# Transposing x in pairs of chunks: two chunks to a PSUM bank, one copy for both, and a new order of all steps

## The chip, the core and the metric

The kernel runs on one core of one Trainium2 chip. The metric is the device time of one execution in microseconds. Three runs of the kernel before took 796.67, 796.89 and 797.10 us. The profile is of one further execution, which took 797.87 us; between its first and last instruction lie 796.0 us. The granted TensorE clock was 1.000 throughout.

The engines are called as in the profile: PE is TensorE (PEld its loads of weights), ACT is ScalarE, DVE is VectorE, POOL is GpSimd, SP is the engine that issues the DMAs.

## What is computed

```python
B, S, D = 1, 2048, 640
xn = layernorm(x)                               # over the last axis
# A: attention with 32 heads of width 20
qkv = xn @ wqkv                                 # [640, 1920]
scores = einsum("bhqd,bhkd->bhqk", q, k) * 20 ** -0.5
s = (softmax(scores) @ v) @ wo
# B: a mixer with two MLPs
h = gelu(layernorm(xn) @ w1)                    # four column groups, shifted by 1, -1, 2, -2 tokens
x1 = xn + shifted(h) @ w2
b = x1 + gelu(layernorm(x1) @ w3) @ w4          # w3 is [640, 1536]
out = x + s * silu(b)
```

All inputs and the output are bfloat16.

## The kernel before

**Tiles.** The 2048 tokens are 16 tiles of 128 tokens, and four chunks `c` (or groups `g`) of 512. The 640 columns of x are five chunks of 128, `kc` 0 to 4. The heads are handled in eight "quads" of four heads, each with four query chunks `qc`. For one quad and query chunk the scores of a key tile are formed for two heads at a time in two PSUM banks (a "score pair", `sc{quad}_{qc}_{tile}_{0 or 1}`, line 1596 or 1609), ACT takes the exponential of the 128x1024 block (`exp...`, line 1656), and PE multiplies the result with the values (`pv...`, lines 1389 and 1588). For a part of the key tiles DVE computes the exponential instead, in bits: `u...` (line 1680) and the pieces `s...` (line 1576, some on POOL, line 1574). The branch B (`w1`, `w2`, `w3`, `w4`), the projections for the next heads (`s1_`, `s0_`) and the final product with `wo` (`woa`, `wob`) are laid into the attention as further PE work whose results DVE evacuates (line 725 is the helper for all of these products).

**A score pair has two forms.** In its row form it is two matmuls of 32 rows by 128 columns (line 1596), in its column form eight of 128 by 32 (line 1609). `follow` (line 218) chooses for the steps that are marked `flex`: the row form when the PE step before is in row form, or the next one is row or flex.

**The order.** `program` only lists the steps. Which engine runs which step when, and which PSUM bank and which buffer each one gets, stands in the string `TABLE`: two characters name a step, and one more character follows for each bank or buffer that it takes. `follow` reads it, keeps the order of the steps of each engine, and adds waits for the buffers. Durations and latencies in the list of steps (`dlat`, `C_SP` and the like) change nothing in the instructions that are emitted except, at most, which of several implied waits is written down.

**PSUM.** Seven banks are handed out: single ones as "W" (for transposes, projections, `wo`), pairs as "S" (score pairs for ACT), any two as "S2" (for DVE). Bank 7 collects the attention output.

**The start.** x is loaded and normalised (DVE, ACT and POOL share the tiles). PE transposes x on itself: for a group of four tiles and a chunk `kc`, sixteen matmuls of 128x128 (line 1076, steps `tr_x{g}_{kc}_{tile}` of four matmuls each) fill half a PSUM bank with 512 bfloat16 columns, and one copy (line 1085, steps `trev_x{g}_{kc}`) brings them to `xnT`:

```python
for kc in range(0, 0 if g in cfg.TD else cfg.KC, cfg.TP):
    h, wa = self.wtile()
    act = bk in cfg.TRA
    bk += 1
    nk = min(cfg.TP, cfg.KC - kc)
...
    def fe(e, d=d, h=h, nk=nk, act=act):
        p = self.wbank(h, BF16)[:, 0:512 * nk].rearrange("p (k n) -> p k n", k=nk)
        return e.activation(d, p, AF.Copy) if act else e.tensor_copy(d, p)
```

`cfg.TP` is 1, so there are 20 such banks and copies, numbered `bk` 0 to 19; `cfg.TRA` lists the 14 that ACT copies, DVE copies six. The key projection of group c, `KT_c` (five steps of four matmuls), needs the chunks of group c alone. DVE takes its largest absolute value (`mx_c`, line 1177) and ACT brings it to SBUF (`kev_c`, line 1180). Only when all four are there, DVE combines the maxima (`mx_`, `mq_`, lines 1192 and 1194), and PE adds the bound to the queries (`sh_0`, line 1161; `qad_0`, line 1167). Then come the first score pair and the first exponential. Until the first chunks are there, PE runs 41 fillers (`warm`, line 898).

**The end.** The last query chunk of the last quad is done in two halves of 256 queries (`sh0_`, `sh1_` are its score pairs, lines 1467 and 1471; `exph0_`, `exph1_` their exponentials; `uh0_`, `uh1_` DVE's, line 1506). The rows of the output that wait for the last quad alone are `wob8` to `wob15` (line 1827), each filling two banks which DVE empties (line 1834). `keep_busy` (line 1411) lays filler matmuls into PE's queue there, 29 steps; `cfg.FLN` lists their form (0: four matmuls, 1: two in row form) and number.

Of the kernel before, what the change touches and what calls it, by code (L numbers as in the profile page):

```python
# [472 lines left out]
class Cfg:  # L473
# [5 lines left out]
    def __init__(self, S=2048, D=640, H=32, F=1536):  # L479
# [48 lines left out]
        self.OND = 100.0  # L528
        self.TP = 1
# [125 lines left out]
class Gen:  # L655
# [29 lines left out]
    def A(self, name, *key):  # L685
        a = (name,) + key
        self.pl.own(name, a)
        return a
# [1337 lines left out]
    def b_w3(self, c0):  # L2026
# [8 lines left out]
        for ch in (c0, c0 + 1):  # L2035
# [12 lines left out]
            for fc in range(FC):  # L2048
# [3 lines left out]
                  writes=[A("W3s", ws)], is_dma=True, nbytes=KC * 128 * 128 * 2, name=f"ld_w3_{ch}_{fc}", stream=f"w3{ws}")  # L2052
# [16 lines left out]
    def b_w4(self, n0, n1):  # L2069
# [6 lines left out]
        for hh in range(2):  # L2076
            hs = slice(hh * HALF, (hh + 1) * HALF)
            T("sp", C_SP, lambda e, hs=hs: e.dma_start(W4[:, :, :], w4src[:, :, hs]),
              writes=[A("W4")], is_dma=True, nbytes=FC * 128 * D, dlat=800.0, name=f"ld_w4_{n0 // 4}_{hh}", stream="w4")
# [27 lines left out]
    r"#6#9#0#y#:###,#$#-$@$K$V#f#(#)$)#;#<#=#>#%#e$b#&#?#@#A#B#C&c#'#*&d#.#D#E#F$*#G$2#H$+$,#I$-$.#n#}#~$/#J$##K$0#g$3$4%5)#z#{#|#L#M#N#+#O#P#Q#d#R$$#S#s$%%"  # L2107
    r":##r$5#k$c#T$&#p#o#U#t#V$'#W$6#X#q#Y#u#i#Z$M$P$d$1$L#v#w#x$n$$o$p$s%$x(#m%&&%'%($($}'$~$t$u$7$v$8$9$N%#%$$:$O$;%%$Q$q$r$e$g$<$R$?%)$w#h#[$D#]$y#^$z$E$"
    r"{#_%*#`$|#a&b#b&e$%w%%x$f$>$A&l'&m&z&%y%z&{$B$F&n$S$C%{&o%+(&p$=$h$G$i#j$Z&|$X%|&}$H%6%7%8%9%,%;%<%=$W&~%>%-&f%.&g%/%0%&h&i%1$[#l%2$j%3%4$I$k%?)%@%A$]"
    r"%~#$Y%B%C&#$T$l#c$^$J&$&%&&$U%X%$_%Y%N(%O%P%S)%Z%[%]%T%U&q%V$m%D'%E'#&)&&j&*%I$%Q&+(X%F%G%W%J&,%K$`%c%%R%H$a%L&-%^)%_%`%a%h(%d%i%j&'%e%f%k%b#2%r'%s%l%"  # L2110
    r"t%u%m)%n%o%p%M&0$&1&2&3&4%g%v%q&.&7%&8%}&/&9(Y&5&:&6&;'+'&<','-'.'/&O&&>&?&@&('0&F$&D(#8&G&H&E1l&I&J&K*:&*;%&P&Q&=*G(*<)*H#*>*=&R&S*J$*@/&T*B*K$*?(*A%"
    r"&s&&t&u&v&w*L%&X)&Y*E(*M&*C&x&y#/*P+*S*R&Z&[&]'u*F'*T%*N*V('%#'&&^&_*k(''*l&*U**h%*W'(')*i$*D*m(*n)*I'1&'2'*'8#*O%'9*Q%&A&L':';'<*X#5*f('=*g#&U&M)&N+A"
    r"'3*r%*s''4'5*o+%&*z(#7'6'7*j'Y&'Z'[']'^+&)*[&`('$&a*{#'K''L'M*p&*q$*e'N'O*|('?(*}&'@'A'_'>'P*w#+#&'B+$%'C*_&V%*x('D&W'R$'S'T'U'V*~'W+($+)#+C'+F*Y*]+E+"
    r"/#*t+0&+4(+5$+H$'E#+J'F'G*b'H+K+*#++''I*c1m'J&C+'+-$+9(+:)'f#'g'h'i*^+,'j'k+.%'l*u#+S(*Z+V+U'`#'a'b'c+7$'d*v#*y+G#'e+8'+X(+Z'm#+I#+[&B+M$*a'n+1(W+t#+w"
    r"(Z+N(+2(+3%'o'p'q+B$'r's+O(+v+y/+6+{*d+D&+;+R$+W#+P$+Y)*`+T%([+|'t'v#'w'x+<,V+=+k(+i#'y'z+Q+j'+b+l$'|('}'{'~(#($+s#+x&+L+h+z(+u)(%(&%('+m,-4,'&((()(*,"
    r"(#+_,/'X,G#,H&+d(+(,((-+~&,0,2(,#$,)#,5,*'(.(/,4(0.},$&,%%(1(3+}+],c#,D((^((2+e+f(_+`+g,E)+>+^,+(a,d(&r,X&,Z+n(+o#,B#,C',&+c+a,^$,I(,J$,>,6,[+p#,F,a,7"
    r"+q%,L',`,1$(5$(6(7(8,;,K,=(9,3),i#,,$,@,M',8,:,N'(:'Q,?+r,.$,<,]$+?+@,l,O&,k,n1,q,_#,p,A,m',o),P(](`,9,Q(;$-)$,W#,Y$(<,t-*%(=,r(>(?(@,s,e#,R,h',b,w,j&"
    r",f#,u,z(A((B,v--6-9'-0-:$(C(D(E-'#-j-(',},g-$'-/-26(F-4(G(-%)(H(j-1#-3#-5(I)*(J(K-7(-8&-<&-+-=%(k&(l(m(L-B%-E-D,~(-#',{(n(o(p->&,|.7%-G(-I-&-?(.8)-;,y"
    r"-J-,&-M(M-.&-@,x-P-A#-F(-L(d((e-H$(f(c(P-C%(g(h(i-K-W&(b(4-6-Q)+&(N),)--X'-Z%-[#).)/)0-N-l&-n-`(-a&-O-Y-V-o-b#-q$-t-s-R-]((O#-c$-^'(Q-p#-S-d(R-T-|$-~-"
# [115 lines left out]
```

## Time and profile before

| | |
|---|---|
| median of three runs | 796.89 us |
| the profiled execution | 797.87 us, its span 796.0 us |
| PE busy | 776.3 us (98%) |
| ACT busy | 766.7 us (96%), of which line 1656 676.4 us |
| DVE busy | 730.8 us (92%) |
| POOL busy | 354.5 us (45%) |
| copies of the transposed x on ACT (line 1085) | 14, 7.4 us |
| copies of the transposed x on DVE (line 1085) | 6, 2.3 us |

Busy time of PE is modelled from pipelined matmuls, and overlapping ones make it look full; whether PE waits is read from the waits of its weight loads (PEld). A row of the timeline gives start, length, engine, line, operation, tiles and count, then in brackets the idle time before it and what ended that. In the rows of waits the three numbers are the total, the count and the longest wait.

### The profile page before, as it was taken

What the parts mean: (1) busy time and instruction counts of PE and PEld (TensorE: products, weight loads), DVE (VectorE), ACT (ScalarE), POOL (GpSimd) and SP (SyncE); (2) the same over time, 40 slices, a digit from 0 to 9 for tenths busy, and PEclk for the clock granted to TensorE, in tenths of its full rate; (3) what the DMA queues carried; (4) which work ended last, traced back from release to release, by engine and by line L of the source; (5) the groups of instructions that cost most, each with busy time, mean ns of one, the idle gap of its engine ahead of it and who ended that gap; (6) DMA issues with size and microseconds to landing.
All of it is one profiled execution on the core that took longest, in us unless ns stands there. A gap on an engine that the chain in (4) does not pass through costs nothing.

```text
span 796.0 us, 29830 instructions
## 1 busy us (share of the span) xinstructions
PE 776.3 (98%) x13369; PEld 322.5 (41%) x13369; DVE 730.8 (92%) x1206; ACT 766.7 (96%) x802; POOL 354.5 (45%) x208
## 2 busy tenths in 40 slices
PE   9999999999999999999989999999999999999997
PEld 4433333334444333333534444334333343435454
DVE  8889899999999999999998999999988888999967
ACT  7899999999999999999999999999999999999994
POOL 5464234242546737663443442544232443442553
PEclk9999999999999999999999999999999999999999
DMA  5013552444031214335141143314242112133522
GB/s 166 11 24 82 132 121 63 109 111 92 9 68 37 48 40 81 84 75 102 37 101 44 23 104 54 79 43 85 57 97 67 21 43 67 24 91 82 144 90 85
DMA packets 138671, 57.58 MB, mean 72 GB/s; under 512 B 111040, under 2 KB 133744, under 8 KB 138544
## 3 DMA queue, kind: packets, MB, share of 16 engines
q1 hardware_dynamic: 138544, 55.68, 30.2%
q8 instruction: 105, 1.72, 0.9%
q14 instruction: 22, 0.18, 0.1%
HBM read 34.70 MB, written 10.33 MB: 57 GB/s over the span
## 4 chain that ended last, share of the span: by engine, by line
ACT 55%; PE 40%; DVE 3%; issue 1%; DMA 0%; SPq 0%; DVEq 0%
ACT arena L1656 47%; PE psum L725 13%; PE psum L1596 9%; PE psum L1588 6%; PE psum L1389 5%; PE psum L1609 4%; ACT arena L2063 3%; ACT arena L1638 2%; PE psum L898 2%; DVE arena L1680 1%; ACT arena L1971 1%; ACT arena L2091 1%; PE psum L1076 1%; PE psum L1467 1%; ACT L1656 0%
## 5 line engine op out<-in xcount | busy, mean ns | idle before, releaser
L1656 ACT ACTIVATE arena<-psum 128x1024 bf16<-128x1024 f32 x726 | 676.4, 1040 | 13.8 <-PE psum L1596 8.5
L1680 DVE TENSOR_SCALAR arena<-psum 128x512 uint16<-128x512 f32 x536 | 341.6, 682 | 27.9 <-PE psum L1596 24.3
L1574 POOL TENSOR_TENSOR arena<-arena 128x2048 int32<-128x2048 int32 x68 | 244.5, 3599 | 263.8 <-DVE arena L1576 178.7
L725 PE MATMUL psum<-arena 128*32 128x320 bf16 (+1 forms) x5776 | 327.5, 332 | 2.1 <-DVE arena L1576 1.7
L1596 PE MATMUL psum<-arena 32*128 32x512 bf16 x1642 | 197.2, 384 | 7.7 <-ACT arena L1656 4.5
L725 PEld LDWEIGHTS psum<-arena 128*32 128x32 bf16 x5776 | 140.4, 96 | 121.1 <-issue 26.3
L1588 PE MATMUL psum<-arena 128*22 128x512 bf16 x2144 | 183.5, 381 | 1.0 <-DVE arena L1708 0.9
L1576 DVE TENSOR_SCALAR arena<-arena 128x4096 uint16<-128x4096 uint16 (+1 forms) x151 | 161.3, 1090 | 3.7 <-PE psum L1588 2.9
L1389 PE MATMUL psum<-arena 128*22 128x512 bf16 x1448 | 137.8, 381 | 0.3 <-DVE arena L1708 0.2
L1596 PEld LDWEIGHTS psum<-arena 32*128 32x128 bf16 x1642 | 55.0, 91 | 177.8 <-ACT arena L1656 97.5
L1609 PE MATMUL psum<-arena 128*32 128x512 bf16 x1368 | 104.1, 381 | 0.1
L1588 PEld LDWEIGHTS psum<-arena 128*22 128x22 bf16 x2144 | 50.0, 91 | 61.3 <-issue 29.4
L1716 POOL TENSOR_TENSOR arena<-arena 128x512 bf16<-128x512 f32 x30 | 40.9, 1363 | 63.3 <-DVE arena L1576 45.9
L1389 PEld LDWEIGHTS psum<-arena 128*22 128x22 bf16 x1448 | 35.7, 90 | 48.0 <-issue 24.4
L1609 PEld LDWEIGHTS psum<-arena 128*32 128x32 bf16 x1368 | 28.6, 95 | 34.6 <-ACT arena L1656 25.3
L2056 DVE CAST arena<-psum 128x512 bf16<-128x512 f32 x48 | 32.7, 683 | 3.9 <-PE psum L725 3.4
L1265 DVE CAST arena<-psum 128x512 bf16<-128x512 f32 x40 | 26.9, 684 | 1.7 <-PE psum L725 1.2
L1638 ACT ACTIVATE arena<-psum 128x2048 bf16<-128x2048 f32 x13 | 24.5, 1888 | 0.6 <-PE psum L1596 0.6
L937 DVE BATCH_NORM_STATS2 arena<-arena 128x6 f32<-128x320 bf16 x54 | 24.3, 478 | 0.7 <-DMA arena<-in_A_x_dram 0.7
L954 POOL TENSOR_SCALAR arena<-arena 128x640 bf16<-128x640 bf16 x16 | 14.0, 877 | 24.2 <-DVE arena L1576 20.2
L1708 DVE STREAM_TRANSPOSE arena<-psum 128x512 f32<-128x512 f32 x31 | 22.0, 709 | 1.4 <-PE psum L1588 1.4
L2063 ACT ACTIVATE arena<-arena 128x6144 bf16<-128x6144 bf16 x4 | 21.1, 5315 | 0.0
(125 smaller groups left out, 360.4 us busy)
## 6 DMA issues: line engine op xcount, KB each, us to landing
arena<-in_B_w_dram SPq DMA_DIRECT2D x48, 160.0 KB, 2.8
arena<-arena SPq DMA_DIRECT2D x124, 32.0 KB, 1.9
arena<-in_B_w_dram SPq DMA_DIRECT2D x4, 960.0 KB, 6.6
arena<-in_A_x_dram SPq DMA_DIRECT2D x8, 320.0 KB, 5.8
arena<-in_A_x_dram SPq DMA_DIRECT2D x16, 160.0 KB, 2.5
out_dram<-arena SPq DMA_DIRECT2D x16, 160.0 KB, 2.0
heads<-arena SPq DMA_DIRECT2D x120, 20.0 KB, 2.0
arena<-queries SPq DMA_DIRECT2D x28, 80.0 KB
```

The costliest lines, as they stand in the source:

```text
L725: ins = e.matmul(pb[32 * c:32 * c + 32, 0:N], lhsT(k, c), rhs(k, c), start=(k == 0), stop=(stop and k == nk - 1), tile_position=(0, 32 * c))
L1389: ins = e.matmul(pb[32 * i:32 * i + 22, 0:512], VA[:, ql, kts[i // 2], i, :], PT[:, slots[i // 2][0].slot, 512 * (i % 2):512 * (i % 2) + 512],
L1574: return e.tensor_tensor(dst.bitcast(I32), U[:, ub, 0:w].bitcast(I32), bass.AP(c.tensor, c.offset, [list(c.ap[0]), [0, w // 2]]), op=ALU.add)
L1576: fa if onp else lambda e, v=v, dst=dst: e.tensor_scalar(dst, U[:, ub, 0:w], EXP_B[v], None, op0=ALU.add),
L1588: ins = e.matmul(pb[32 * i:32 * i + 22, 0:512], wv, dst[:, at:at + 512].bitcast(BF16), start=first, stop=final, tile_position=(0, 32 * i))
L1596: return e.matmul(out, self.KT[32 * i:32 * i + 32, b, 128 * kt:128 * kt + 128], self.QT[32 * i:32 * i + 32, b, 512 * qc:512 * qc + 512], s ...
L1609: ins = e.matmul(out[32 * c:32 * c + 32, :], self.KT[:, b, 128 * kt + 32 * c:128 * kt + 32 * c + 32], self.QM[:, gb, 2 * a + jj, :], start ...
L1638: lambda e: e.activation(self.PT[:, hp[0].slot:hp[0].slot + 2, :], self.psum[:, 512 * h0.slot:512 * h0.slot + 2048].rearrange("p (a b) -> ...
L1656: lambda e: e.activation(self.PT[:, hp.slot, :], self.psum[:, 512 * hs.slot:512 * hs.slot + 1024], AF.Exp, scale=cfg.scale),
L1680: lambda e, k=k, h=h: e.tensor_scalar(U[:, ub, 1024 * at + 512 * k:1024 * at + 512 * k + 512], self.bank(h.slot)[:, :], a_exp, EXP_BIAS, o ...
L1716: return e.tensor_tensor(OnT.rearrange("p (k d a) -> p a k d", k=4, a=4), Ob[:, :].rearrange("p (a k d) -> p a k d", a=4, k=4), in1, op=AL ...
L2063: T("act", c_act(FC * 512), lambda e, G=G, i=i: e.activation(G[:, i, :, :], G[:, i, :, :], AF.Gelu_apprx_tanh), reads=gta, writes=gta, nam ...
```

## The change

- `TP` becomes 2: in each group the chunks 0 and 1, and 2 and 3, share a bank, and one copy of 128x1024 takes both to SBUF; chunk 4 keeps a bank and a 128x512 copy of its own. 12 copies are left, `bk` 0 to 11. `TRA` gives 1 to 8 of them to ACT (five of 1024 columns, three of 512), so DVE has `trev_x0_0` and the three of group 3 (three of 1024, one of 512).
- `FLN` lists 31 fillers in place of 29, in other forms.
- `TABLE` is another string: every engine's queue is ordered anew, and banks and buffers are handed out anew. Apart from the copies and the fillers, the steps are the same.
- `W3L`, `W4L` and `OND` are latencies that stand in the list of steps; the first two keep their values.

```diff
@@ class Cfg
         self.OND = 100.0
+        self.W3L = 0.0
+        self.W4L = 800.0
         self.TP = 1
...
         self.OQ = 1800.0
+        self.OND = 800.0
         self.WF = True
-        self.FLN = tuple( [(0, 1), (0, 2), (1, 3), (0, 5), (1, 2), (1, 2), (1, 3), (0, 11)])
+        self.TP = 2
+        self.TRA = [1, 2, 3, 4, 5, 6, 7, 8]
+        self.FLN = tuple( [(0, 2), (1, 4), (0, 3), (1, 2), (1, 2), (1, 3), (1, 1), (0, 3), (0, 11)])
...
@@ b_w3, b_w4
-                  ..., is_dma=True, nbytes=KC * 128 * 128 * 2, name=f"ld_w3_{ch}_{fc}", stream=f"w3{ws}")
+                  ..., is_dma=True, nbytes=KC * 128 * 128 * 2, dlat=cfg.W3L, name=f"ld_w3_{ch}_{fc}", stream=f"w3{ws}")
...
-              ..., is_dma=True, nbytes=FC * 128 * D, dlat=800.0, name=f"ld_w4_{n0 // 4}_{hh}", stream="w4")
+              ..., is_dma=True, nbytes=FC * 128 * D, dlat=cfg.W4L, name=f"ld_w4_{n0 // 4}_{hh}", stream="w4")
...
@@ TABLE: every line of the string but the first few characters differs
```

The queues of the start, read from the two strings (banks are not shown, and stretches that don't matter here are left out; `x0_4` and the like after the first of a run are `trev_x0_4` and so on):

```
ACT before  trev_x0_1 x0_4 x0_2 | sxx15 norm6 norm5 qev_0 | trev_x1_2 x1_3 x1_0 x1_1 x1_4 | norm14 | trev_x2_4 x2_3 x2_2 x2_0 x2_1 | trev_x3_3 | kev_1 kev_2 kev_0 kev_3 | exp...
ACT after   trev_x0_4 x0_2 | sxx15 norm6 norm5 qev_0 | trev_x1_4 | norm14 | trev_x1_0 x1_2 | trev_x2_4 x2_0 x2_2 | kev_0 kev_1 kev_2 kev_3 | exp...
DVE before  ... norm12 norm13 mx_0 | trev_x3_0 qbias x3_2 x3_1 x3_4 | mx_1 aq_0 ve2 mx_2 mx_3 mx_ mq_ vev0_5 qad_0 ...
DVE after   ... mx_0 norm12 norm13 vev0_3 | trev_x3_2 x3_4 x3_0 | aq_0 mx_1 mx_2 mx_3 mx_ mq_ qbias vev0_5 qad_0 ...
PE before   ... KT_1 and the transposes of groups 2 and 3, mixed; KT_2 KT_3 | v0_5 | QT_2_0 QT_1_0 | sh_0 ...
PE after    ... transposes of group 2 | KT_1_0 to KT_1_3 | transposes of group 3 | KT_1_4 KT_2 KT_3 | QT_1_0 QT_1_1 v0_5 QT_1_2 | sh_0 ...
```

In the middle, all queues keep their broad course (the same exponentials, the Gelu and the output steps come after the same number of exponentials to within a few) and differ in the fine order nearly everywhere.

The queue of PE at the end, from the score pairs of the last half on, with the pair of banks each takes:

```
before   sh1_14a1:[3,4] sh1_14a0:[0,1] wob8:[3,4] sh1_12a0:[0,1] sh1_1d1:[3,4] wob9:[0,1] sh1_12a1:[3,4] sh1_10a0:[0,1] wob10:[3,4] wob11:[0,1] sh0_8a0:[3,4] sh1_1d0:[0,1] sh0_8a1:[3,4] sh1_10a1:[0,1] ...
after    sh1_14a0:[5,6] sh1_14a1:[0,1] wob8:[5,6] sh1_12a0:[0,1] sh1_1d1:[5,6] sh1_12a1:[0,1] wob9:[5,6] wob10:[0,1] sh1_10a0:[5,6] wob11:[0,1] sh0_8a0:[5,6] sh1_1d0:[0,1] sh0_8a1:[5,6] sh1_8a1:[0,1] ...
```

More of the change, by code (lines that the diff above doesn't have):

```diff
@@ L2111 @@
[L2111 to L2114, printed above, removed]
@@ L2199 @@
[L2199 to L2200 removed]
+    r"$)#9#,$@#y#6$K&Z#%##&[#&#f$2$1$b$3#(#)#-#.#$#e$*#'#:#;$+$,$-#<#=#>#*#?#@#z#A#B#C#g#D$.#}$4#E#F$/#G#+#H#d#{#I#n#J#K$0#L%)##~#|#k$##M#N$$#s#O#P$%#p#Q$&$"
+    r"(#r#i#R#S$5$6$c$'#o$7#T$d#t#q#l#U#/$P#V#W#X#u#v#Y$M$L#Z#[#]#^#_$8#`$9#w%$$#x$w%$:$n&$N$;%%$o$O$p#h$e$x$E%&%'$q$r$s$t$y$z${%($|$Q$g$u$R$}$<$S$~$v%#$B#m"
@@ new lines @@
+    r"R)dx)bSa.a'd1#d)e1d2#d7'd3%bL$bTd8$bUbMbNbVbWbObPbQd5#d6&dyc~d-&cJd.'a(`tc}cNa5bZa6cKeP#eQ)d+d*d9d&d'eA&d#eR(eS$d(d4bb&eB&bcb['bdbee+bfbgeC(bXbjb]b^b_"
+    r"eD#b`e9&bYe:%d%bad/eEeJ#eL(d$eK#eM&bq#brbsbh^*e.btbubz)b{bve7#b|b}bye8(d:bib~c#eN#e<(e='edbk)d;ble(d<e>#bmbnbobpey(e?)ez$e,d>d?e{#eOc$)e*d=d^(c%c&c'c("
+    r"e|#e;bwd_c)et#eV(eWeu(c*d@dAdBdCev#e/ew&db(e@e0e'e}df#dceo(ep)d`c+e)ddexdedgdhdDdEdFdj#dkdle-dibxdme2(e3'dGdHeT#eUdIdJe4(e5(dKdLdMel#em#dNej(e6e&eaece"
+    r"k$e^e`eq#eFer%eg$eGe_eneHeIdOdPdQf&(eZee#eYeh$eXf'e[f*$f(e]esdaebef#eif+e~f#f$f%f,f-f)dRdSdTdUdVdWdXdYdZd[d]f.#f2$f/f3f0f1f4f5f6")
```

182 lines of the change are left out of this document (90 added, 92 removed).

## The prediction

> **What bounds the kernel now.** I read the page first, then the busy time by stage, the waits, and last the chain and the timeline at both ends.
>
> ```profile
> PE 776.3 (98%) x13369; PEld 322.5 (41%) x13369; DVE 730.8 (92%) x1206; ACT 766.7 (96%) x802; POOL 354.5 (45%) x208
> ```
>
> ```profile
> 40.00:764.00 724.00, 712.79 (x12006) 288.19 (x12001) 674.21 (x1069) 714.00 (x728) 322.71 (x156) 1.00 0.32 71
> 100.00:200.00 100.00, 99.62 (x1582) 37.80 (x1578) 95.19 (x145) 98.00 (x95) 36.68 (x16) 1.00 0.41 98
> 200.00:300.00 100.00, 99.15 (x1734) 41.90 (x1726) 98.17 (x172) 96.60 (x104) 56.33 (x27) 1.00 0.20 41
> 600.00:700.00 100.00, 97.69 (x1690) 40.40 (x1686) 90.73 (x138) 99.91 (x100) 39.03 (x14) 1.00 0.20 45
> ```
>
> ```profile
> PEld psum L1596 <- ACT arena L1656: 97.5, 252, 0.8
> ...
> PEld psum L1588 <- issue: 29.4, 126, 0.4
> ...
> ACT arena L1656 <- PE psum L1596: 8.5, 20, 1.3
> ```
>
> In a row by stage the third busy figure is DVE's, the fourth ACT's. From 40 to 764 us ACT is busy for 714.0 of 724 us. It stands for 10.0 us: 2.0 between 100 and 200, 3.4 between 200 and 300, 0.1 between 600 and 700. PE looks as full, but its loads for score pairs wait 252 times, 97.5 us in all, until ACT has freed a bank, while ACT waits for a score pair 20 times, 8.5 us. ACT sets the pace, and its exponentials are not changed. In the middle a new order can give at most the 10.0 us; it can lose more. Beyond that, time can come only from an earlier first exponential or from the end.
>
> **The start.** The chain of waits and the timeline before the first exponential:
>
> ```profile
> 20.47 0.32 PE psum L898
> ...
> 23.80 1.12 PE psum L1076 x72
> 24.92 0.62 issue
> 25.54 0.24 PE psum L1076 x4
> 25.78 2.18 PE psum L725 x40
> ...
> 27.99 0.70 DVE arena L1177
> ...
> 28.71 0.17 DVE arena L1192
> ...
> 28.90 0.25 DVE arena L1194
> ...
> 30.91 9.25 ACT arena L1656 x10
> ```
>
> ```profile
> 18.64 2.55 ACT L1085 ACTIVATE arena<-psum 128x512 bf16<-128x512 bf16 x5
> ...
> 24.50 1.09 DVE L1085 COPY arena<-psum 128x512 bf16<-128x512 bf16 x3
> ...
> 26.11 0.28 DVE L1154 TENSOR_SCALAR arena<-arena 128x512 uint16<-128x512 uint16 x1
> ```
>
> The transposes of group 3 end at 25.78 (0.62 us of it a stop of PE that nothing in the profile explains), PE then runs KT_2 and KT_3 without a break to 27.96, and DVE takes KT_3's maximum and the bound (until 29.15). 1.76 us later comes the first exponential. That last stretch keeps its steps, so what the change is worth here is how much earlier 29.15 comes.
>
> A copy of 512 columns costs ACT 0.51 us (2.55 for 5) and DVE 0.36 (1.09 for 3). ACT's copy of 1024 should cost what its exponential of 1024 from PSUM costs, 0.94 (11.27 for 12, row below). For DVE's copy of 1024 I take the same ratio, 0.36 x 0.94 / 0.51 = 0.66; its bounds are 0.36 (free) and 0.72 (nothing shared).
>
> [...]
>
> ACT's copies fall from 14 x 0.51 = 7.1 us to 5 x 0.94 + 3 x 0.51 = 6.2; DVE's go from 6 x 0.36 = 2.2 to 3 x 0.66 + 0.36 = 2.3. Neither sum is on the path by itself: ACT has its copies of group 2 done before PE asks for KT_2, in both orders. What counts is the last group. In the new order DVE alone copies it: chunks 2 and 3, then 4, then 0 and 1, whose transposes are PE's last. PE gets there earlier by KT_1_4, which now follows the transposes (2.18 / 10 = 0.22 a step), and by a filler that stood in between and now stands earlier (0.32): 25.78 - 0.54 = 25.24, if the stop of 0.62 stays. Then DVE: last copy 25.3 to 25.96, the absolute values of the queries (0.28) to 26.2, three maxima of 0.70 to 28.3 (PE has KT_3 ready at 25.24 + 11 x 0.22 = 27.7, so DVE waits no more), the bound (0.17 + 0.25) at 28.75. That is 0.4 us before 29.15. Bounds: 1.0 earlier if PE's stop goes too; 0.6 later if DVE starts its three copies only when all the transposes are done (25.3 + 1.68 in place of 25.96).
>
> [...]
>
> **The end.** ACT's queue from the last halves on, and DVE's two longest evacuations there:
>
> ```profile
> 764.27 11.27 ACT L1656 ACTIVATE arena<-psum 128x1024 bf16<-128x1024 f32 x12
> 776.03 1.02 ACT L1656 ACTIVATE arena<-psum 128x1024 bf16<-128x1024 f32 x1 [0.49 <-PE psum L1467]
> 778.28 2.04 ACT L1656 ACTIVATE arena<-psum 128x1024 bf16<-128x1024 f32 x2 [1.23 <-PE psum L1467]
> 781.42 1.03 ACT L1656 ACTIVATE arena<-psum 128x1024 bf16<-128x1024 f32 x1 [1.09 <-PE psum L1467]
> 782.93 5.74 ACT L1656 ACTIVATE arena<-psum 128x1024 bf16<-128x1024 f32 x6 [0.49 <-PE psum L1467]
> ```
>
> ```profile
> 775.25 0.82 DVE L1834 SCALAR_TENSOR_TENSOR arena<-psum,arena 128x640 bf16<-128x640 f32 x1 [1.11 <-PE psum L1827]
> ...
> 776.57 1.23 DVE L1506 TENSOR_SCALAR arena<-psum 128x1024 uint16<-128x1024 f32 x1
> ```
>
> Here all runs through two pairs of banks, filled by PE and emptied by ACT (0.94) or DVE (0.82 for `wob`, 1.23 for `uh`), with about 0.5 us to refill (the waits of 0.49). ACT stands for 0.49 + 1.23 + 1.09 + 0.49 = 3.3 us, the long ones where both pairs are with DVE. In the new queue one pair has `wob8`, `sh1_1d1`, `wob9` in a row, all DVE's, and the other two exponentials in a row. Walked with the same prices, from 774.6: 0.5 + 0.82 + 0.5 + 1.23 + 0.5 + 0.82 + 0.5 = 779.5 until `exph1_10_0` can start, while ACT is through with the other pair at 778.5. So ACT stops 0.49 twice, then 1.0, then 0.49 twice as the pairs alternate: 3.0 in place of 3.3, a gain of 0.3, of which I take 0.2. Bounds: 3.3 less at best, 1 more at worst. The last exponential, DVE's normalisation and the two last `wob` keep their places. The two further fillers stand behind the last score pairs or where PE waits for banks: nothing, and 0.4 us if that wait were gone.
>
> **The middle.** No row shows the new order here, so it is bounded from both sides. Read from the string, ACT's and DVE's steps are the same in number; PE has the same 785 of 966 flexible score pairs in row form, and changes between the forms 776 times, not 782. A change costs PE a gap like the 0.23 us (29.4 for 126) before line 1588. Six are 1.4 us of PE, and as PE is ahead most of the time I count half, -0.7. Of 739 exponentials 471 had no other exponential between their score pair and themselves in the string, so ACT may find them late; now 448, 5% fewer: of the 10.0 us, -0.5. Bounds: all 724 us as between 600 and 700 would be 0.7 us idle, a gain of 9; all as between 200 and 300 would be 25, a loss of 15.
>
> **SP's queue.** The loads of the next heads' keys (`fKT1`) move up behind their store (`dk1_0`), which issues near 70 us; SP waits there until it has landed, and behind it stand the load of the masked queries for chunk 3 (`qm0_3`) and those for the w1 branch.
>
> ```profile
> keys<-arena SPq DMA_DIRECT2D x4, 480.0 KB, 4.7
> ```
>
> ```profile
> 82.23 3.47 SPq L1356 DMA_DIRECT2D arena<-arena x4
> ```
>
> Before, `qm0_3` is issued at 82.23; chunk 3's first score comes some 80 exponentials after the first, at 31 + 80 x 0.94 = 106. 4.7 us of waiting is covered by that; without the cover it would be 4.7.
>
> **The sum**, against the profiled execution's own 797.87 us (0.98 above the median of the runs): -0.4 - 0.2 - 0.7 - 0.5 = -1.8, so 796.1 there, and 795.1 for a run like the median of 796.89. 0.2%, about what a measurement of this kernel can tell from no change, is 1.6 us.
>
> **The rivals.**
> 1. *DVE becomes the bound of the start.* Its copies of group 3 queue up behind the last transposes, 0.6 later instead of 0.4 earlier, and the middle gives half of what I count, -0.6 with the end's -0.2 on top: 796.89 + 0.6 - 0.8 = 796.7, no difference. For it: in the row of 24.50 three of DVE's copies do stand back to back. Against: in the new queue only the last copy needs the last transposes. 0.22.
> 2. *The new order lets ACT wait in the middle: slower.* Three engines are full between 100 and 300, and a score pair that PE issues some 0.5 us later than ACT needs it cannot be made good. If ACT stands all along as it does from 100 to 200, 2.0 in 100 us, that is 14.5 us in place of 10.0: 796.89 + 4.5 - 0.6 (start and end) = 800.8. It decides from an idle time above 10.0 + 1.6 + 0.6 = 12.2 us between 40 and 764. For it: the order differs nearly everywhere, and 97.5 us of PE's waits show how little is kept in hand. Against: the counts above are a little better, not worse. 0.30.
> 3. *The middle becomes as smooth as its best stretch in half of it:* -5 in place of -1.2, 791.3. Within "faster", 0.1 of its 0.48.
>
> **How the numbers follow.** My forecast, 795.1, is the likeliest with 0.38; its own range is 793.3 to 796.0 (end and start at their nearer bounds). With the third rival faster has 0.48, same 0.22, slower 0.30. The cases of both signs hold most of the chance, so the range goes from 791.5 to 800.6, just short of the priced ends on both sides.
>
> **What would show it right or wrong.** Right: line 1085 with 8 copies on ACT of 0.5 and 0.9 us and 4 on DVE; the first exponential near 30.5 us, with DVE's maxima back to back before it; ACT idle of at most 10 us between 40 and 764; four or five stops of ACT after 775, 3 us in all. Wrong: a first exponential after 30.9, with DVE's copies of group 3 starting only after PE's last transpose; or an idle time of ACT above 12.2 us in the middle, with waits on line 1596 or on a DMA that were not there.

## The result, and the profile after

The changed kernel takes 796.2 us (median of 22 runs, 794.9 to 797.8), the kernel before 798.1 in the same session (22 runs, 796.7 to 800.1). The ratio is 0.9975, with a 95% interval of 0.9967 to 0.9983: 1.4 to 2.6 us faster. The profiled execution took 796.42 us, its span 794.7 (before 797.87 and 796.0). Two executions of all those below, one of e1 at 3689 us and one of the kernel before at 1793 us, are left out of the ratios.

The busy figures of the changed kernel, first from its page, then by stage:

```profile
PE 775.4 (98%) x13373; PEld 322.1 (41%) x13373; DVE 731.4 (92%) x1204; ACT 765.8 (96%) x796; POOL 353.6 (44%) x208
```

```profile
40.00:764.00 724.00, 714.39 (x12018) 287.67 (x12014) 676.16 (x1071) 714.54 (x729) 320.91 (x155) 1.00 0.32 71
...
400.00:500.00 100.00, 99.47 (x1754) 41.42 (x1746) 95.33 (x153) 99.37 (x107) 38.23 (x21) 1.00 0.32 65
```

The same stage of the kernel before:

```profile
400.00:500.00 100.00, 97.99 (x1736) 40.87 (x1728) 93.34 (x148) 98.17 (x105) 38.63 (x22) 1.00 0.32 65
```

ACT (the fourth busy figure) stands for 9.5 us between 40 and 764, where it stood for 10.0. But the half microsecond is not spread thin: between 400 and 500 alone it won 1.2, and it lost elsewhere, 0.9 of it between 700 and 764. The experiments will show one stop that went and one that came.

The start of the changed kernel, by the chain of waits and by DVE's timeline:

```profile
22.61 1.12 PE psum L1081 x80
23.73 0.16 PE psum L730
23.89 1.11 issue
25.00 3.88 PE psum L730 x71
...
29.26 0.76 DVE arena L1172
...
30.52 10.20 ACT arena L1661 x11
```

```profile
23.19 1.62 DVE L1090 COPY arena<-psum 128x1024 bf16<-128x1024 bf16 x3 [1.14 <-PE psum L1081]
...
25.44 0.69 DVE L1182 TENSOR_REDUCE arena<-psum 128x1 f32<-128x512 f32 x1 [0.43 <-PE psum L730]
26.52 0.69 DVE L1182 TENSOR_REDUCE arena<-psum 128x1 f32<-128x512 f32 x1 [0.39 <-PE psum L730]
27.60 0.69 DVE L1182 TENSOR_REDUCE arena<-psum 128x1 f32<-128x512 f32 x1 [0.39 <-PE psum L730]
```

The transposes of group 3 are done at 23.73, two microseconds earlier than before. Then PE stops for 1.11 us, for nothing that the profile names (0.62 before), and DVE's last three maxima each wait 0.4 us for PE's next product: PE sets the pace here, not DVE. The first exponential comes at 30.50 (before 30.89).

ACT's queue at the end:

```profile
763.83 10.53 ACT L1661 ACTIVATE arena<-psum 128x1024 bf16<-128x1024 f32 x11 [0.95 <-PE psum L1472]
774.95 1.02 ACT L1661 ACTIVATE arena<-psum 128x1024 bf16<-128x1024 f32 x1 [0.58 <-PE psum L1472]
776.46 1.02 ACT L1661 ACTIVATE arena<-psum 128x1024 bf16<-128x1024 f32 x1 [0.49 <-PE psum L1472]
778.60 1.02 ACT L1661 ACTIVATE arena<-psum 128x1024 bf16<-128x1024 f32 x1 [1.12 <-PE psum L1476]
780.11 1.02 ACT L1661 ACTIVATE arena<-psum 128x1024 bf16<-128x1024 f32 x1 [0.49 <-PE psum L1472]
781.62 5.69 ACT L1661 ACTIVATE arena<-psum 128x1024 bf16<-128x1024 f32 x6 [0.49 <-PE psum L1472]
```

After 774 ACT stops five times, 3.2 us in all (four times, 3.3 us, before). New is the stop of 0.95 that ends at 763.83.

Between the two profiles lie 1.3 us of span, not the 1.9 of the runs: 0.4 come from the first exponential, 0.7 from ACT's idle time between the first exponential and the last (0.5 in the middle, 0.1 at the end), 0.3 from ACT's instructions being a little shorter.

### The profile page after: what moved, and what is told of

Its sections match the earlier page's. It is cut to its first block, busy times and chain, and to the rows that moved or that the text cites. A ratio compares the mean times of both kernels' runs of the same rounds, so it can differ in the third digit from the quotient of the medians.

```text
span 794.7 us, 29817 instructions
## 1 busy us (share of the span) xinstructions
PE 775.4 (98%) x13373; PEld 322.1 (41%) x13373; DVE 731.4 (92%) x1204; ACT 765.8 (96%) x796; POOL 353.6 (44%) x208
## 4 chain that ended last, share of the span: by engine, by line
ACT 48%; PE 47%; DVE 3%; DMA 1%; issue 1%; DVEq 0%
ACT arena L1661 42%; PE psum L730 16%; PE psum L1601 10%; PE psum L1593 8%; PE psum L1394 5%; PE psum L1614 5%; ACT arena L2068 3%; ACT arena L1643 1%; PE psum L903 1%; ACT arena L1976 1%; DVE arena L1685 1%; DMA arena<-in_B_w_dram 1%; PE psum L1081 1%; ACT arena L2096 1%; PE psum L1472 1%
## 5 line engine op out<-in xcount | busy, mean ns | idle before, releaser
L1581 DVE TENSOR_SCALAR arena<-arena 128x4096 uint16<-128x4096 uint16 (+1 forms) x151 | 163.0, 1101 | 3.2 <-PE psum L1593 2.6
L1884 POOL TENSOR_TENSOR arena<-arena 128x640 bf16<-128x640 bf16 x12 | 17.0, 1427 | 14.8 <-DMA out_dram<-arena 6.1
L1340 POOL TENSOR_SCALAR arena<-arena 128x176 bf16<-128x176 bf16 x20 | 7.1, 360 | 36.1 <-DVE arena L1581 16.7
```

The costliest lines, as they stand in the source:

```text
L1581: fa if onp else lambda e, v=v, dst=dst: e.tensor_scalar(dst, U[:, ub, 0:w], EXP_B[v], None, op0=ALU.add),
```

## Experiments: start or rest?

The two orders can be spliced: one kernel's queues up to some exponential, then what is left of the other's, in its order. Each comparison below is with the kernel before, timed beside it.

**e1: the changed start alone.**

```
changed order up to exp0_0_3_1 (TP = 2, 12 copies) | order and fillers of the kernel before
```

> The changed kernel's queues up to the fourth exponential (pairs of chunks, 12 copies), and from there on the queues and fillers of the kernel before; eight exponentials get another buffer. Theory 1, the gain is the sum of a start and a rest that do not depend on each other: the start gives 0.4 us, so 0.9995 of before; first exponential at 30.5 us, PE's stop of 1.1 us again after its matmul 478; ACT idle between 40 and 764 us as before (10 us), 3.3 us of stops at the end. Rival, the new order of the rest is worth nothing and all of the gain comes from the start: 0.9975 of before.

Measured: 1.0036 (1.0021 to 1.0051), slower, as neither theory had it. ACT's timeline shows a part of the reason:

```profile
31.27 3.79 ACT L1661 ACTIVATE arena<-psum 128x1024 bf16<-128x1024 f32 x4 [1.40 <-PE psum L1601]
36.40 3.90 ACT L1661 ACTIVATE arena<-psum 128x1024 bf16<-128x1024 f32 x4 [1.34 <-PE psum L1601]
```

Where the two orders meet, ACT stops for 1.34 us, which neither kernel has there: the splice has a price of its own. It is about half of the 2.9 us lost; what the other half is isn't shown. And the first exponential came at 31.27, not at 30.5.

**e2: the changed rest alone.**

```
order of the kernel before up to exp0_0_3_1 (TP = 1, 20 copies) | changed order and fillers
```

> The other half: the start of the kernel before (20 copies) up to its fourth exponential, then the queues and fillers of the changed kernel; ten exponentials get another buffer. Theory 1: the rest gives what is left, 1.0 to 1.5 us, so 0.998 to 0.9987 of before; first exponential at 30.9; ACT idle between 40 and 764 about 9.4 us. Rival, the rest is worth nothing: 1.000.

Measured: 0.9992 (0.9980 to 1.0003), which contains both outcomes. This splice has a price too: ACT stops for 0.48 us until 34.33, which neither kernel has there. The first exponential came at 30.07, 0.8 earlier than in the kernel before, whose start it has. So one profile's first exponential says little: the first transposes, too, come sooner or later (11.91 us here, 12.44 in the kernel before). What can be compared is the way from the first transposes of group 0 (the row of 68 or 80 transposes near 12 us in PE's timeline) to the first exponential:

| profile | transposes | first exponential | between |
|---|---|---|---|
| before | 12.44 | 30.89 | 18.45 |
| e2, start of before | 11.91 | 30.07 | 18.16 |
| e5, start of before | 11.55 | 30.63 | 19.08 |
| e9, start of before | 12.47 | 30.58 | 18.11 |
| after | 12.26 | 30.50 | 18.24 |
| e1, changed start | 13.21 | 31.27 | 18.06 |
| e6, changed start | 12.43 | 30.27 | 17.84 |
| e8, changed start | 13.31 | 31.02 | 17.71 |
| e11, changed start | 13.17 | 31.23 | 18.06 |

The old start takes 18.45 us in the mean of four, the new one 17.98 in the mean of five: 0.47 less, with ranges that overlap. The first column spreads by 1.8 us.

**e8: the changed order for the first 100 us**, with a splice where the orders nearly agree.

```
changed order up to exp0_2_13_1 | order and fillers of the kernel before
```

> The changed kernel's queues for the first 100 us (to the exponential exp0_2_13_1), then those of the kernel before; one exponential gets another buffer. The joint of e1 cost a stop of 1.36 us by itself; here the two orders have all but 13 steps in common at the joint. Theory 1, the start gives nothing that can be measured: counted from the first transposes of group 0, the first exponential comes after 17.4 us as in the kernel before (17.4 to 17.7), and ACT's idle time is that of before, so 0.9995 to 1.0003. Rival, the start is worth the 0.4 us that the two profiles differ by, or more: 0.9990 or less.

Measured: 1.0007 (0.9993 to 1.0021); 17.71 us between (by this count the kernel before has 18.45, not the 17.4 expected). ACT stops for 0.40 us at the splice, until 103.20. By the table the start is worth a few tenths of a microsecond; in the time this can't be told from nothing.

## Experiments: the stop in the middle

Before, between its exponentials 378 and 379, ACT stood for 1.28 us, because PE was late with a score pair:

```profile
419.67 1.94 ACT L1656 ACTIVATE arena<-psum 128x1024 bf16<-128x1024 f32 x2 [1.28 <-PE psum L1596]
```

```profile
418.09 0.59 PE L725 MATMUL psum<-arena 128*32 128x320 bf16 x12 [1.70 <-DVE arena L1576]
```

All profiles with the old order there show this stop (e1 1.03, e8 0.83), and none with the new order does. PE's row at that place, in e8:

```profile
418.09 0.59 PE L730 MATMUL psum<-arena 128*32 128x320 bf16 x12 [1.25 <-DMA arena<-in_B_w_dram]
```

Here PE's wait is put down to the landing of a load. In the kernel before it is put down to a DVE step (line 1576), which ended at the same moment.

**e5: one score pair moved ahead of the waiting work.**

```diff
  PE queue of the kernel before
+ sc4_0_8_0
  w4_1_0_0 w4_1_0_1 w4_1_0_2
  pv4_0_b0
  w4_1_0_3 ... w4_1_0_11
- sc4_0_8_0                    (stood behind w4_1_0_5)
```

> The kernel before with one step moved: the score pair sc4_0_8_0 stands ahead of the twelve steps of w4_1_0 and pv4_0_b0 in PE's queue, not in the midst of them (the pair before it and itself swap forms by that). Theory 1, what the new order gave in the middle is one stop: before, ACT stands 1.28 us at its exponential 379 (419.67 us), because this pair is behind work that waits 1.70 us for DVE (line 1576); the changed order has none there. So the stop goes or shrinks to 0.3 or less, ACT's idle time between the first and the last exponential falls from 13.35 to about 12.2 us, and the time to 0.9984 to 0.9990 of before. Rival, the next pair is late in its place: the stop comes back one or two exponentials later, 1.000.

Measured: 0.9996 (0.9985 to 1.0008), and ACT stops 0.89 us at the same exponential. The theory fell: the pair took the column form and still came late. PE's wait was now put down to the load of w4, `ld_w4_0_0`. So I looked at SP's queue. Before:

```profile
410.22 0.39 SPq L2078 DMA_DIRECT2D arena<-in_B_w_dram  x1
411.84 1.42 SPq L1286 DMA_DIRECT2D arena<-keys  x4
```

and in the changed kernel:

```profile
409.43 0.40 SPq L2083 DMA_DIRECT2D arena<-in_B_w_dram  x1
409.86 0.80 SPq L1262 DMA_DIRECT2D arena<-in_A_wqkv_dram  x1
410.71 1.71 SPq L1272 DMA_DIRECT2D queries<-arena  x1
```

Before, the fetch of the next keys (`fKT5`) follows the load by 1.62 us; in the changed order it comes some 80 exponentials later, and another load (160 KB) and a store (480 KB) follow the load of w4 instead, within 1.3 us. The last number in the rows of DMA issues is the time to landing; the load before:

```profile
arena<-in_B_w_dram SPq DMA_DIRECT2D x1, 960.0 KB, 7.7
```

and in the changed kernel:

```profile
arena<-in_B_w_dram SPq DMA_DIRECT2D x1, 960.0 KB, 5.3
```

**e9: the fetch of the keys two steps later**, all else as in the kernel before.

```diff
  SP queue of the kernel before
  ld_w4_0_0
- fKT5
  on3_2
  dk0_3
+ fKT5
```

> The kernel before with one step of SP's queue moved: the fetch of the keys for quad 5 (fKT5, four DMAs of 80 KB) stands behind the next two steps (on3_2 and the store dk0_3), 2.5 us later, in place of right behind the load of w4 (ld_w4_0_0, 960 KB). Theory 1: ACT's stop at its exponential 379 is the landing of that load. Before, it is issued at 410.22, the fetch follows at 411.84 and the load takes 7.7 us; in the changed order another, smaller load and a store follow it, it takes 5.3 us, and there is no stop. Here it should land in 5.3 to 6.3 us, PE's wait ahead of w4 (1.70 us in the profile of before, 1.45 and 1.25 in e1 and e8, which have the same stretch) go to 0.3 or less, ACT's stop of 1.28 (1.03, 0.83) to 0.2 or less; first to last exponential 0.8 to 1.2 us shorter, 0.9985 to 0.9990 of before. Rival, the store dk0_3 (480 KB) delays the load as much as the fetch does: landing 7 us or more, the stop stays at 0.8 or more, 1.000.

Measured: 0.9978 (0.9969 to 0.9988). SP's queue, the landing, ACT's timeline and the stage in e9:

```profile
411.01 0.39 SPq L2078 DMA_DIRECT2D arena<-in_B_w_dram  x1
...
414.15 2.78 SPq L1286 DMA_DIRECT2D arena<-keys  x4
```

```profile
arena<-in_B_w_dram SPq DMA_DIRECT2D x1, 960.0 KB, 5.6
```

```profile
413.55 11.13 ACT L1656 ACTIVATE arena<-psum 128x1024 bf16<-128x1024 f32 x12
```

```profile
400.00:500.00 100.00, 99.63 (x1754) 41.33 (x1758) 94.85 (x151) 99.50 (x106) 39.95 (x23) 1.00 0.32 65
```

The load lands after 5.6 us, ACT runs through the place without a stop, and the stage looks like that of the changed kernel. One step of one queue, with PE's, ACT's, DVE's and POOL's queues untouched, gives what the whole change gives, within the intervals. The upper end of the saving (2.5 us) is more than the stop; the lower (1.0) is not. The profile alone would not have shown it: from the first exponential to the last, e9 takes 757.10 us where the kernel before takes 757.78, only 0.68 less, because ACT lost 0.8 us between 100 and 200, where nothing was moved. By that much one execution differs from another; it takes the many runs to see one stop.

**e11: the other way round**, in the changed kernel.

```diff
  SP queue of the changed kernel
  ld_w4_0_0
  ld_ws4_0
+ fKT5
  dk0_3
...
- fKT5                         (some 80 exponentials later)
```

> The changed kernel with one step of SP's queue moved the other way round than in e9: the fetch of the keys for quad 5 (fKT5), which the changed order issues some 80 exponentials later, stands right behind the loads ld_w4_0_0 and ld_ws4_0, as in the kernel before. Theory 1 (the gain of the middle is the landing of the load of w4): the load, issued at 409.4, lands after 7 to 8 us in place of 5.3; PE wants it at 415.9 and waits 0.7 to 1.5 us; ACT has a stop of 0.5 to 1.2 us near exponential 379 that the changed kernel doesn't have, and the time goes back to 0.9985 to 0.9995 of before. Rival, in the changed order enough score pairs stand ahead of w4 to cover a late load: a wait of PE, but no stop of ACT over 0.2 us, 0.9975.

Measured: 0.9986 (0.9974 to 0.9999), which contains both outcomes. In the profile there is no stop near 379. SP's queue and the landing:

```profile
410.14 0.40 SPq L2083 DMA_DIRECT2D arena<-in_B_w_dram  x1
...
412.65 1.48 SPq L1291 DMA_DIRECT2D arena<-keys  x4
```

```profile
arena<-in_B_w_dram SPq DMA_DIRECT2D x1, 960.0 KB, 5.4
```

The fetch has to wait for the last score pairs of the quad before, and came 2.51 us behind the load, not 1.62; the load landed in time. So this run did not bring back the situation that it was to test, and neither theory is refuted by it; that the fetch brings the stop back in the changed order is not shown. Over all profiles the picture is sharp: with the fetch 1.62 us behind, the load took 7.7, 7.5, 7.3 and 7.2 us (before, e1, e8, e5); with it 2.51 or 3.14 us behind, 5.4 and 5.6 (e11, e9); with it far away, 5.2 to 5.6 (after 5.3, e2 5.2, e6 5.5, and five others). Distance alone can't be the reason: in the changed order a load of 160 KB and a store of 480 KB follow closer than the fetch does before, and the load of w4 lands in 5.3 us. Why this fetch costs two microseconds at 1.6 us and nothing at 2.5 stays open.

## Experiments: PE's stop in the start

Counting PE's queue, the stop came after 477 matmuls in the kernel before, amid transposes, and after 478 in the changed one, inside `KT_1_4`. A smaller one (0.21 us at 20.91) lies 128 matmuls ahead of it, after 350. The page has, among the DMA queues,

```profile
q8 instruction: 105, 1.72, 0.9%
```

packets and MB: 16.4 KB each, and 13373 matmuls to 105 packets are 127 to a packet. (The matmuls are counted as the trace has them; a few records can be missing, and in e2 and e9 the count at the stop is 475.)

**e3: 20 fillers fewer ahead of the transposes.**

```diff
-        self.NPF = [41, 0]
+        self.NPF = [21, 0]      # 9, 9 and 3 where 19, 19 and 3 stood
```

> The changed kernel with 21 fillers before the transposes in place of 41 (9, 9 and 3); all else as it is. Theory A, PE's stop belongs to a place in its stream of instructions, which comes in blocks of 128 matmuls: in the kernel before it stands after matmul 477, in the changed one after 478 (and a small one 128 earlier, after 350), though other work stands there. With 20 matmuls fewer ahead the stop moves 20 matmuls down the program, into KT_2, and the one of 350 into the last transposes of group 2; more slow matmuls then stand between the two, so the stop shrinks to 0 to 0.6 us, and the first exponential comes at 29.3 to 30.0 us in place of 30.5. Theory B, the stop belongs to the step KT_1_4, where something that the trace does not show is late: 1.1 us at KT_1_4 again, first exponential at 30.5. If PE runs its transposes slower after the pause that now stands ahead of them, the chunks of group 0 come later and the first exponential after 30.5.

Measured: 0.9975 (0.9963 to 0.9986), as the changed kernel. The chain of waits:

```profile
22.57 1.12 PE psum L1081 x80
23.69 1.26 PE psum L730 x21
24.94 0.83 issue
25.77 2.80 PE psum L730 x51
```

The stop moved exactly 20 matmuls down the program (21 products behind the transposes where there was 1) and so stands after matmul 477 of the trace, where it stood after 478: theory A. It shrank less than hoped, to 0.83, and 17.74 us lie between transposes and first exponential (30.19 less 12.45), which puts the first exponential later than the 29.3 to 30.0 expected. The records of the packets of queue q8 show how it comes about:

| | PE passes matmul 350 | packet starts | packet has landed | PE goes on behind 478 |
|---|---|---|---|---|
| before | 22.05 | 22.80 | 24.16 | 25.54 |
| after | 21.12 | 22.84 | 23.79 | 25.00 |
| e3 | 21.36 | 22.91 | 24.31 | 25.77 |
| e6 | 21.11 | 22.16 | 23.28 | 24.76 |
| e7 | 20.49 | 21.33 | 22.29 | 23.51 |

In each row PE goes on 1.2 to 1.5 us after the packet has landed, and the packet starts 0.8 to 1.7 us after PE has passed the border before. The six other profiles with this stop (e1, e2, e5, e8, e9, e11) have the same 1.3 to 1.5 us. So these 128 matmuls took 3.0 to 4.4 us from border to border, while 128 transposes alone would take 1.8 (128/80 of 1.12). The stop itself was 0.27 to 0.95 us with the old start (before, e2, e5, e9) and 0.83 to 1.11 with the new one (after, e1, e6, e8, e11), which comes to matmul 350 sooner (21.12 in the changed kernel, 22.05 in the kernel before). That the stop ends with what the packet of 16.4 KB brings is read from these times and from the count of 127 or 128 matmuls to a packet; what is in a packet, no trace shows.

In the profile of e3 the end lost what the start had won. Its stage 782 to 789, where the sixth figure behind the length is the granted clock:

```profile
782.00:789.00 7.00, 6.89 (x113) 4.03 (x115) 4.45 (x10) 5.04 (x6) 0.00 (x0) 0.51 0.17 58
```

The clock is halved for 6.8 us, PE gets 113 matmuls done where the changed kernel has 175 in the same stage, and ACT stands for 1.6 us there.

**e7: float32 fillers**, so that PE has no pause.

```diff
-            return e.matmul(..., self.wz[:, 0:128], self.wz[:, 0:512], ...)
+            return e.matmul(..., self.Ob[:, 0:128], self.Ob[:, 0:256], ...)   # float32, 21 of them
```

> The changed kernel with 21 fillers of 256 float32 columns in place of 41 of 512 bfloat16 columns (10, 9 and 2): as few instructions as with 21 fillers, but PE has no pause before the transposes. Theory A (PE's stream of instructions comes in blocks of 128 matmuls): the stop stands after matmul 477 or 478 again, 20 further on in the program than in the changed kernel, inside KT_2; the first exponential comes 0.3 us earlier in relation to the first transposes of group 0. Theory C, the granted clock that fell to 0.5 from 782 to 789 us with 21 plain fillers (2.1 us lost at the end) follows from the pause: no fall here, 0.994 to 0.996 of before. Rival, it follows from the number of instructions or is chance: the fall is there again, 0.9975. If a float32 filler counts as several instructions, the stop stays where it is in the changed kernel.

Measured: 0.9985 (0.9971 to 0.9999), short of the 0.994 to 0.996 of theory C. The trace has 42 matmuls ahead of the transposes, two for each filler, and the stop stood at `KT_1_4` again, as the last sentence had it; it was 0.42 us, with the packet landed at 22.29, where the changed kernel's landed at 23.79. Only 16.96 us lay between transposes and first exponential (29.02 less 12.06), and the clock did not fall; both are one profile, and the time doesn't confirm them. The mean granted clock of an execution speaks against the pause. It was 0.995 in the profile of e3, with its fall. It is 0.996 or less in four of the twelve executions of e7, which has no pause, in four of the twelve of e3, and in five of the twelve of e6, with 41 fillers. For the changed kernel it is four of 22, for the kernel before one or two of 21 to 35 beside each set of experiments. The profile of e12, again with 41 fillers, shows a fall as well, to 0.5 for 3.4 us from 782.3 on. What makes the clock fall, and whether the changed order makes it fall more often, stays open.

**e10: whole transposes**, 80 matmuls in place of 320 (on top of e6, below).

```diff
-                            for c in range(4):
-                                ins = e.transpose(pb[32 * c:32 * c + 32, o:o + 128], xn[:, n, kc * 128 + 32 * c: ...], ..., tile_position=(0, 32 * c))
+                            return e.transpose(pb[:, o:o + 128], xn[:, n, kc * 128:kc * 128 + 128], self.ident[:, :])
```

> The changed kernel with the two steps of e6 (loads moved back), and each transpose of 128x128 as one matmul in place of four of 128x32: 80 matmuls in place of 320, so 240 fewer ahead of the first exponential. Theory A (PE's instructions come in blocks of 128 matmuls, and a block that is run in less than about 3.5 us makes PE wait for the next): blocks end after matmul 94, 222 and 350 of the kernel's own; 222 now falls into the transposes of group 3, with over 5 us of work since 94, and 350 behind the first exponential. So there is no stop of over 0.3 us between the first transposes of group 0 and the first exponential, which comes 16.8 to 17.2 us after them (17.7 to 18.2 in the four profiles with the changed start), DVE's copies and maxima being next in line; 0.9960 to 0.9968 of before. Rival: a whole transpose takes longer than four quarters side by side (0.056 us for the four): at 0.1 us the 40 of groups 2 and 3 cost 1.8 us more and the gain is lost, 18.0 to 19.5 us, 0.9975 to 0.9990.

Measured: 0.9981 (0.9965 to 0.9996). The chain of waits, and DVE's timeline:

```profile
22.79 0.98 PE psum L730 x16
23.77 1.22 PE psum L1080 x20
24.99 3.81 PE psum L730 x76
```

```profile
24.41 1.62 DVE L1086 COPY arena<-psum 128x1024 bf16<-128x1024 bf16 x3 [0.99 <-PE psum L1080]
...
26.15 2.08 DVE L1178 TENSOR_REDUCE arena<-psum 128x1 f32<-128x512 f32 x3
```

No stop is left between the transposes and the first exponential: theory A once more. But the gain is gone, as the rival had it (18.0 to 19.5 us, 0.9975 to 0.9990), though not for the rival's reason. PE came to `KT_1_4` at 24.99, where the changed kernel went on at 25.00. From the first value projection (15.03; 14.76 there) that is 9.96 us of work without a stop, where the changed kernel needs 8.97 to the same step with its 0.21 in it. A whole transpose costs no more than four quarters: by the two chains of waits, six, seven and three whole ones behind quarter matmuls take 0.44, 0.50 and 0.27 us, their quarters in the changed kernel 0.34, 0.39 and 0.17, always 0.10 or 0.11 less, whatever their number. It is the change between whole and quarter matmuls that costs PE 0.10 to 0.12 us (the eight products behind the three take 0.47 us from start to start, 0.35 in the changed kernel), 13 times here. DVE now runs its three maxima back to back: with PE's stop gone, DVE is the bound that the prediction had expected. 18.00 us in all (30.44 less 12.44).

**e12: three value projections whole as well.**

```diff
+                if whole is not None:        # v0_0, v0_1, v0_3
+                    return e.matmul(pb[:, 0:N], whole(k), rhs(k, 0), start=(k == 0), stop=(stop and k == nk - 1))
```

> The kernel of e10 (loads moved back, transposes of 128x128 as one matmul), and the three value projections v0_0, v0_1 and v0_3 that stand among the transposes as whole matmuls of 128x320 too, in place of four of 32 columns each: of 14 changes between whole and quarter matmuls after the first transposes of group 0 four or more go. Theory: e10 lost to the changes (0.2 us each) what it won by having no stop for instructions. Then the first exponential comes 17.0 to 17.5 us after the first transposes of group 0 (18.0 in e10), and the time is 0.9968 to 0.9978 of before. Rival, a whole matmul is slower by its own weights' load (98 ns for 128 columns): 17.8 or more, nothing over e10.

Measured: 0.9968 (0.9956 to 0.9980), the lowest ratio of all, and 17.66 us between transposes and first exponential (30.62 less 12.96): better than e10, short of the 17.0 to 17.5 expected, for which a change was to cost 0.2 us. Between whole projections the six and seven transposes take 0.34 and 0.39 us, as the quarters do; the three, with quarter products behind them, take 0.26 (0.27 in e10): the price of the change once more. Its interval overlaps that of the change (0.9967 to 0.9983), so it is not shown to be faster than the changed kernel.

## Experiments: the copies, and a collision at the end

**e4: the pairing undone, the order kept.**

```diff
-        self.TP = 2
-        self.TRA = [1, 2, 3, 4, 5, 6, 7, 8]
+        self.TP = 1
+        self.TRA = [2, 3, 4, 5, 6, 7, 8, 9, 10, 11, 12, 13, 14]   # a pair's second copy behind its first
```

> The changed kernel's order with the pairing undone: each chunk has a bank and a copy of 512 of its own again (20 copies), a pair's second copy right behind the first on the same engine; all else as in the changed kernel. Theory 1, the copies are not on the path, PE is: first exponential at 30.5 us (within 0.1), time as the changed kernel's, 0.9975 of before. Rival, the smaller number of copies is what brings the first exponential forward: 30.9 or later, 0.998 to 0.9985 of before.

Measured: 1.0020 (1.0011 to 1.0029), and the first exponential at 33.23, 21.31 us after the transposes: worse than either theory. The chain of waits:

```profile
21.72 0.39 PE psum L1079 x26
...
22.12 2.56 ACT arena L1088 x5
...
25.78 0.32 PE psum L1079 x21
...
26.13 1.76 DVE arena L1088 x5
```

PE runs its transposes of groups 2 and 3, and at the key projection behind each it waits, 1.90 us for ACT's copies of group 2 and 0.81 for DVE's of group 3 (and 1.70 earlier, at 19.47, for a DVE step). The first of these projections, `KT_1`, reads no chunk of group 2; what it can lack is the bank: with one for each chunk the seven banks run out. That is read from the order of the waits, not tested by itself. In this order the pairs are needed not for fewer copies but for fewer banks. The kernel before, which mixes its transposes with other work, gets along with single copies.

**e6: two steps of SP's queue back where the kernel before has them** (in part: its load comes first, too).

```diff
  SP queue of the changed kernel
+ ld_xr3
+ st_out1
  ld_xr4
  st_out2
- ld_xr3
- st_out1
```

> The changed kernel with two steps of SP's queue moved: the load of x for tile 3 and the store of tile 1 (ld_xr3, st_out1) stand ahead of ld_xr4 and st_out2 again, as the load does in the kernel before. Theory 1: in the changed kernel's profile POOL's addition for tile 3 (line 1884, 1.40 us) starts at 760.48, so late because of that load, and DVE's piece of 4096 that starts at 760.70 takes 2.26 us where 1.21 is usual; ACT stops 0.95 us at 763.83. With the load earlier POOL is through before 760.5, the piece takes 1.2 and the stop goes: 0.9988 of the changed kernel, 0.9960 to 0.9968 of before. Rival, the long piece is chance or has another cause: 2.2 us again, time as the changed kernel's.

In the changed kernel POOL and DVE at this place:

```profile
760.48 1.40 POOL L1884 TENSOR_TENSOR arena<-arena 128x640 bf16<-128x640 bf16 x1 [2.19 <-DMA out_dram<-arena]
```

```profile
760.70 3.40 DVE L1581 TENSOR_SCALAR arena<-arena 128x4096 uint16<-128x4096 uint16 x2 [1.33 <-PE psum L1593]
```

and in e6:

```profile
758.02 1.40 POOL L1884 TENSOR_TENSOR arena<-arena 128x640 bf16<-128x640 bf16 x1
```

```profile
760.56 2.36 DVE L1581 TENSOR_SCALAR arena<-arena 128x4096 uint16<-128x4096 uint16 x2 [1.33 <-PE psum L1593]
```

Measured: 0.9975 (0.9961 to 0.9989). POOL is through before DVE begins, the two pieces take 2.36 us in place of 3.40, and ACT has no stop at 763. (The row of the changed kernel puts POOL's wait down to a store; e6 moves a store and a load, so which of the two held it isn't told.) With the changed order ACT stopped there in four profiles of six (after 0.95, e3 0.95, e7 0.69, e11 0.67; not in e2 and e4), with the two steps moved in none of three (e6, e10, e12). In the time 0.95 us that come in some executions only are not to be seen. In the four profiles with the stop the first piece took 2.26, 2.27, 2.00 and 1.99 us (1.23 in the kernel before and in e6), and each time it ended 1.08 or 1.09 us behind the end of POOL's addition. So the long piece goes with the late addition; why it is longer beside it, no run shows.

## Why the prediction was right, and where it was right for another reason

- **The sum.** Forecast -1.8 us; measured -1.9 (1.4 to 2.6). The time itself, 796.2, is 1.1 above the forecast 795.1 and just outside its own range (793.3 to 796.0), because the forecast started from three runs with a median of 796.89 and the 22 have 798.1. That ACT's line 1656 sets the pace and that only its 10.0 us of idle time, the start and the end could give anything was contradicted by no experiment. But of the steps that make up the sum, two failed, and that it came out is in good part luck.
- **The start, -0.4.** The size was right (0.39 between the two profiles, 0.47 between the means). The step that failed is the one that kept PE's stop of 0.62 "that nothing in the profile explains" as a constant and made DVE the bound. The transposes ended at 23.73, not 25.24; PE's stop grew to 1.11, because PE passed matmul 350 sooner (21.12 against 22.05) and the packet started no sooner (22.84 against 22.80); and DVE waited for PE, so the sign "DVE's maxima back to back" did not come. That the bound was ready at 28.76 (28.75 forecast) is luck: by the prediction's own numbers the two were a tie, DVE at its third maximum at 27.6 and PE's product ready at 27.7. The prices of the copies held nearly: the three of group 3 took DVE 1.62 us (1.68 forecast); a double copy has a mean length of 0.69 us on DVE (0.66 forecast) and 1.02 on ACT (0.94), where the forecasts are costs in a row without gaps, in which copies overlap a little (three of 512 columns on DVE took 1.09 us in a row in the kernel before, where its six have a mean length of 0.41).
- **The copies off the path.** True of their time, but the prediction didn't look at the banks that they hold. e4: undone in this order, the pairs cost 3.3 us of the start (21.31 against 17.98).
- **The end, -0.2.** 3.3 us of stops became 3.2; walked by hand they came to 3.0. Right in size, at the edge of what can be told.
- **The middle, -0.7 for six changes of form and -0.5 for the pairs just ahead of their exponential.** The size came out near by luck, the step was wrong. 10.0 us less the stop of 1.28 leave 8.7; 9.5 less the new stop of 0.95 leave 8.5. Apart from these two stops, the reordering of PE's, ACT's and DVE's queues was worth 0.2 in these two profiles, not 1.2; the other profiles differ among each other by more (without the two stops 8.3 to 9.3 with the old order, 8.4 to 9.3 with the new). The 1.28 came from SP's queue, and e9 gets it with none of the rest. The prediction walked SP's queue at one place (`fKT1`, quad 1) and called it covered, which it was (ACT is busy for all of the 60 us from 40 to 100, in both profiles); it didn't walk it at the load of w4, and not at the last loads of x, where the change lost up to 0.95.
- **The rivals.** DVE didn't become the bound of the start; ACT's idle time stayed under 12.2 us; neither happened. The view that would have given the step away was in the trace of before: a stop of 1.28 us of ACT, with a wait of PE of 1.70 put down to a DVE step, next to a DMA that took 7.7 us, where it takes 5.3 in the changed kernel.

## What to carry to other kernels

When a tuned kernel's order is changed everywhere, don't spread a small gain over many small causes: list the bounding engine's stops one by one, longest first, and follow each to what ended last, the landings of DMAs included; here one stop of 1.28 us was most of the gain that can be traced, and one step of SP's queue made it. A transfer can land later when another is issued shortly behind it (here after 7.2 to 7.7 us in place of 5.2 to 5.6), so look at the time to landing of each load that something waits for, in both orders. And compare starts from an event inside the program, since the first transposes moved by 1.8 us from profile to profile (11.55 to 13.31), four times what the change was worth there.

## What was not expected of the hardware

- PE stops in the start for nothing that it waits for in the profile: 0.3 to 1.1 us in eleven profiles, after the 475th to 478th matmul of the trace whatever stands there, until 1.2 to 1.5 us after a packet of 16.4 KB of the queue q8 has landed. With 240 matmuls fewer (e10) the stop is gone.
- With a fetch of 320 KB issued 1.62 us behind it, a load of 960 KB landed after 7.2 to 7.7 us (before, e1, e8, e5), without it near after 5.2 to 5.6; with the fetch 2.51 us behind (e11), after 5.4. With a load of 160 KB and a store of 480 KB issued 0.43 and 1.28 us behind it, it landed after 5.3 (the changed kernel).
- A DVE piece of 1.23 us (before, e6) took 2.26 when an addition of 1.40 us on POOL had begun 0.22 us ahead of it (the changed kernel), and 1.99 when it had begun 0.50 ahead (e11).
- A change between whole and quarter matmuls cost PE 0.10 to 0.12 us (e10); six transposes of 128 rows by 128 columns took 0.34 us, 0.056 each, in quarters (the changed kernel) and whole (e12).
- The granted clock fell to 0.5 near the end of two profiles, for 6.8 us in e3, where ACT stood for 1.6 us, and for 3.4 us in e12. A longer pause of PE at the start, which e3 has, is not needed for it.
